# Softmax maxima two chunks ahead, and tile factors at the last block, in a convolution with a mixture of experts

## The chip, the core and the metric

The kernel runs on one core of a Trainium2 chip. A core has five engines that work side by side, each with its own queue of instructions: TensorE (PE, with its weight loads shown as PEld), VectorE (DVE), ScalarE (ACT), GpSimd (POOL) and SyncE (SP), which here only issues transfers. The metric is the time of one execution on the device in microseconds. The time before is the median of 3 runs; the profile is of one further execution.

## What is computed

Two layers follow each other. The first is a causal convolution with 7 taps whose weights are given for each position and head and go through a softmax; the second sends each of the 28672 rows to one of 8 experts, a two-layer network with a ReLU between.

```python
# x: (8, 3584, 192), weight_gen: (8, 3584, 8 heads, 7 taps)
w = weight_gen - np.max(weight_gen, axis=-1, keepdims=True)
w = np.exp(w)
w = w / (np.sum(w, axis=-1, keepdims=True) + 1e-09)
out = np.einsum('bshk,bskhg->bshg', w, x_unf)      # 7 shifted copies of x
...
logits = x @ w_gate                                # (28672, 192) @ (192, 8)
expert_idx = np.argmax(logits, axis=1)
gate_w = probs[np.arange(N), expert_idx]           # softmax of the logits
h = np.maximum(x_sorted[lo:hi] @ w1[e], 0.0)       # (rows, 192) @ (192, 1024)
y_sorted[lo:hi] = h @ w2[e]                        # (rows, 1024) @ (1024, 192)
return gate_w[:, None] * y
```

## The kernel before

**Chunks.** The rows are cut into 28 chunks of 1024 (8 rows on each of 128 partitions). For each chunk `load` brings `x_sb` and `w_sb` (three buffers of each) and the convolution runs on DVE. `soft1` takes the maximum over 7 taps on DVE (L323, `mx`), subtracts it on POOL (L324) and takes the exponential on ACT (L325), all in place in `w_sb`; `soft2` sums on DVE (L330, `sm`), scales (L332) and takes the reciprocal (L335); `soft3` multiplies the weights by it into `wp` in PSUM (L342). `taps` then multiplies and adds (L351, L375): for chunks from 3 on these are 7 multiplications and 6 additions, one instruction each, so that with `soft3` a chunk has 14 steps. The generator `sums` (L660) counts them in `n`: squares of the next chunk (ACT, L407) are written at n = 1 and 2, `soft1` of the next chunk at n = 2, and from n = 4 (`SC_AT`) one instruction of `scale` (L416 to L423, which needs the squares) and `soft2` of the next chunk follows each step. Multiplications read `wp` from PSUM; additions read two operands from SBUF.

**From a chunk to the experts' queues.** `split` makes two half-precision parts of the result and transposes them on PE (L471, copied by ACT at L473). `finish` computes the logits on PE, picks the expert and the gate value on DVE (L492 to L544, the last of them `pos`), and `send` scatters the 1024 rows to the experts' queues in HBM with 8 indirect transfers on POOL (L559, `queue<-pl,pos`).

**Tiles.** `choose` picks full tiles of 256, later 384 rows of one expert as soon as a queue has them; what is left after the last chunk goes in tiles of 384, 256, 128 and fewer rows. There are 97 tiles. `fetch` (L711) issues for a tile, on SP, the rows `xt` (L736), the expert's weights `wt` (L738, three buffers, so a tile's weights wait for the second layer of the tile three before it) and the small table `meta` with gate value and row number (L741). `experts` (L747) computes a tile in blocks of inner units: 8 blocks for 384 rows, 4 for 256, 2 for 128, 1 for 64 and fewer. A block is 5 matmuls per 128 inner units (L797), then a ReLU into `hh` on ACT and its remainder `hl`, on DVE (L820) or, for every third tile (n % 3 = 1), by PE and ACT (L806, L810, L812). Between the blocks of a tile stand the second layer's matmuls (L704) of the tile before it. Each 128 rows of that layer end in `o` (L708, ACT), scaled by the tile's factors `fac`, and a scatter to the output on POOL (L559, `out_dram<-o,meta`).

**The factors.** `fac` (L834, ACT, four buffers) is the table's gate value times a constant that lies with the expert's weights. It is written once per tile, after the first block's ReLU, and first read by the tile's `o`, whose instructions are written among the blocks of the next tile.

**Order.** DVE's order is written out by hand (`tc.manual_schedule`): `vector_step` interleaves the remainders `hl`, the route of a chunk, its split and the steps of `sums` by a clock that is kept in the program. The queues of the other engines are laid out when the kernel is built, by a planner that gives an engine its next instruction from those whose data and buffers it takes to be ready. On the chip each engine then takes its queue in that order and waits where the data are not there.

Of the kernel before, what the change touches and what calls it, by code (L numbers as in the profile page):

```python
# [11 lines left out]
F16 = mybir.dt.float16  # L12
# [7 lines left out]
P = 128  # L20
# [11 lines left out]
J = 8  # L32
# [1 line left out]
HELP = 3  # L34
EARLY = 5
STEP = 0.2
REST = 10.0
REST0 = 12.0
HURRY = 0.3
SOON = 4  # L40
BY_PE = 28
REST1 = 6.0
START = 20.0
AHEAD = 7
# [11 lines left out]
T_MAIN = 384  # L56
CIN = 3
T_STEP = 16
SC_AT = 4
SQ = 4  # L60
PROB = 3
TV = 2
# [51 lines left out]
def conv_moe_kernel(ctx: ExitStack, tc: tile.TileContext, x, wgen, w_gate, w1, w2, out):  # L114
# [202 lines left out]
    ssqs = const.tile([P, 2, J // 2], F32, name="ssqs")  # L317
    nc.vector.memset(ssqs, 0.0)

    def soft1(c):  # L320
        k = ch[c]
        mx = cw.tile([P, J * H], F32, name="mx")
        nc.vector.tensor_reduce(mx, k.w, axis=AX.X, op=ALU.max)  # L323
        nc.gpsimd.tensor_tensor(k.w, k.w, mx.unsqueeze(2).to_broadcast([P, J * H, KW]), op=ALU.subtract)  # L324
        nc.scalar.activation(k.w, k.w, AF.Exp)  # L325

    def soft2(c):
        k = ch[c]
# [120 lines left out]
    def low(c):  # L449
        k = ch[c]  # L450
        p16 = k.pl.bitcast(F16)
        h = k.pc or J // 2
        sub_ = dict(op=ALU.subtract)
        for a, b in ((h, J),) if k.pc else ((0, h), (h, J)):
            nc.vector.tensor_tensor(p16[:, a:b, 2 * P:3 * P], k.acc[:, a:b, 0:P], p16[:, a:b, 0:P], **sub_)
            yield 0.0, (b - a) * 0.14 + 0.08
            nc.vector.tensor_tensor(p16[:, a:b, D:D + 64], k.acc[:, a:b, P:D], p16[:, a:b, P:D], **sub_)
            if b < J:
                yield 0.0, 0.4
        k.lsc = rt.tile([P, 1], F32, name="lsc")  # L460
        nc.vector.tensor_tensor(k.lsc, k.isx, gi, op=ALU.mult)
        xg = cw.tile([P, 4 * J, P], I16, name="xg", bufs=SPLITS)
        k.xg = xg.bitcast(F16)
        k.nb = 3 if c < BY_PE else 4
        if c < BY_PE:

            blocks = [(j, n) for j in range(J) for n in range(3)]
            for i in range(0, len(blocks), 8):
                pt = ps_h.tile([P, 8, P], F16, name="ph")
                for m, (j, n) in enumerate(blocks[i:i + 8]):  # L470
                    nc.tensor.transpose(pt[:, m, :], p16[:, j, n * P:(n + 1) * P], idh)  # L471
                    clock[1] += P / 2400.0 + MM
                nc.scalar.activation(k.xg[:, i:i + 8, :], pt, AF.Copy)  # L473
        else:
            nc.sync.dma_start_transpose(xg, k.pl.bitcast(I16).rearrange("p j d -> p (j d)"))
        k.sent = clock[0] + 0.4
        yield 0.0, 0.4

    def logits(c):
        k = ch[c]  # L480
        k.pm = ps_m.tile([P, 512], F32, name="pm")
        k.lp = k.pm[:, 0:J * 2 * E].rearrange("p (j t e) -> p j t e", j=J, t=2)
        for j in range(J):
            for n in range(3):
                nc.tensor.matmul(k.lp[:, j], k.xg[:, k.nb * j + n, :], gw[:, n], start=(n == 0), stop=(n == 2))
                clock[1] += GATE

    def route1(c):
# [157 lines left out]

    def finish(c):

        yield max(0.0, ch[c].sent + (REST1 if c < BY_PE else REST0 if c < SOON else REST) - clock[0])
        logits(c)  # L650
        yield from route1(c)
        ranks(c)
        yield from gate(c)
        yield from places(c)
        send(c)
        if c == NCH - 1:
            pad_queues()
        yield from choose(c)

    def sums():  # L660

        soft1(0)
        x0 = ch[0].x
        nc.vector.tensor_scalar(x0[:, 0:HALO, :], x0[:, 0:HALO, :], inner, None, op0=ALU.mult)
        square(0, 0, J)
        yield 0.6, None
        for d in chain(scale(0), soft2(0)):
            yield d, None
        for c in range(NCH):
            if c + 2 < NCH:  # L670
                load(c + 2)
            n = 0
            side = iter(())
            for cost in taps(c):
                n += 1
                if n <= 2 and c + 1 < NCH:
                    for i in range(4 * n - 4, 4 * n, SQ):
                        square(c + 1, i, SQ)
                yield cost, None
                if c + 1 < NCH:  # L680
                    if n == 2:
                        soft1(c + 1)
                        yield 0.6, None
                    if n == SC_AT:
                        side = chain(scale(c + 1), soft2(c + 1))
                d = next(side, None)
                if d is not None:
                    yield d, None
            for d in side:
                yield d, None  # L690
            yield 0.0, c
# [55 lines left out]
    def experts():  # L747
# [25 lines left out]
        while True:  # L773
            go = yield n, 0.0
            if not go:
                break
            while len(done_) < min(n + 2, len(todo)):
                loaded[len(done_)] = fetch(len(done_))
                done_.append(len(done_))
            T, xt, wt, meta = loaded.pop(n)  # L780
            fac = ffx.tile([P, 4], F32, name="fac", bufs=4)
            hh = ffh.tile([P, NF, T], F16, name="hh", padded_shape=[P, NF, T_MAIN])
            hl = ffh.tile([P, NF, T], F16, name="hl", padded_shape=[P, NF, T_MAIN])
            fg = max(g for g in (1, 2, 4, 8) if g * T <= 512 or g == 1)
            groups = NF // fg
            for t in range(groups):
                if t:
                    yield None, 0.0
                f0 = t * fg
                flush()  # L790
                while len(pend) > 3:
                    low_part()
                ph = ps_h.tile([P, fg, T], F32, name="ph")
                for g in range(fg):
                    f = f0 + g
                    for k, (wc, xc) in enumerate(((0, 0), (0, 2), (O_L0, 0), (O_H1, 1), (O_L1, 1))):
                        nc.tensor.matmul(ph[:, g], wt[:, wc + f * P:wc + (f + 1) * P], xt[:, xc, 0:T],  # L797
                                         start=(k == 0 and g == 0), stop=(k == 4),
                                         skip_group_check=g > 0)
                hv, lv = hh[:, f0:f0 + fg], hl[:, f0:f0 + fg]  # L800
                while subs:
                    subs.pop(0)()
                if (n % 3 == 1 or todo[n][3] < EARLY) and todo[n][3] < NCH - 1:


                    nc.scalar.activation(hv, ph, AF.Relu, scale=SHRINK)  # L806

                    def rest(ph=ph, hv=hv, lv=lv, fg=fg):
                        for g in range(fg):
                            nc.tensor.matmul(ph[:, g], negi, hv[:, g], start=False, stop=True,  # L810
                                             skip_group_check=True)
                        nc.scalar.activation(lv, ph, AF.Relu)  # L812

                    subs.append(rest)
                    clock[1] += T * fg * (6 + 4.5) / 2400.0 + 15 * fg * MM
                else:
                    nc.scalar.activation(hv, ph, AF.Relu)  # L817

                    def lo(ph=ph, hv=hv, lv=lv):
                        nc.vector.scalar_tensor_tensor(lv, ph, 0.0, hv, op0=ALU.max, op1=ALU.subtract)  # L820
                        return (T * fg + 60) / 960.0

                    cost = T * fg * (5 + 4.5) / 2400.0 + 14 * fg * MM
                    clock[1] += cost
                    pend.append((clock[1] + LATE, n, lo))
                if t > 0 or groups == 1:
                    while pend and pend[0][1] < n:
                        low_part()
                    m = -(-left // (groups - t))
                    second(m)  # L830
                    left -= m
                if t == 0:
                    p = min(P, T)
                    nc.scalar.activation(fac[0:p, 0:T // p], meta[0:p, 0:T // p, 0], AF.Copy,  # L834
                                         scale=wt[0:p, O_INV:O_INV + 2].bitcast(F32))
                if t >= 1 and len(done_) < len(todo):
                    m = len(done_)
                    if m <= n + 2 or (todo[m][3] == NCH - 1 and m <= n + AHEAD + 2):
                        loaded[m] = fetch(m)
                        done_.append(m)  # L840
            while subs:
                subs.pop(0)()
            second(10 ** 6)
            prev = l2(T, hh, hl, wt, meta, fac)
            left = -(-T // P) * NF * 3
            n += 1
# [149 lines left out]
```

## Time and profile before

| | |
|---|---|
| time of the runs | 1338.81, 1340.34, 1341.35 us (median 1340.34) |
| time of the profiled execution | 1336.57 us |
| its span, first to last instruction | 1334.9 us |
| PE busy | 1166.3 us (87%) |
| DVE busy | 1044.7 us (78%) |
| ACT busy | 715.4 us (54%) |
| POOL busy | 588.2 us (44%) |
| granted TensorE clock, mean | 0.954 |

Busy time is the union of an engine's instructions; an instruction that waits is not busy. The views group instructions as `line engine operation out<-in`, with buffer numbers left out. In a view of waits a row reads `engine line <- what ended the wait: us in total, times, longest`; in a timeline a row reads `start, duration, engine, line, operation, out<-in, shapes, count`, and in square brackets how long the engine had stood idle before it and what ended that. In the table of busy time by stretch a row reads `from:to length`, then for each engine its busy time and its number of instructions, then the granted clock, the share of the transfer engines and GB/s. `SPq` marks an instruction of SyncE's queue that issues a transfer.

### The profile page before, as it was taken

Reading aid. Unit: us, or ns where it says so; the run is one execution under the profiler, and the core shown is the slowest. Engines: PE = TensorE matmul, PEld = TensorE weight load, DVE = VectorE, ACT = ScalarE, POOL = GpSimd, SP = SyncE. Lnnn points to the kernel's source line nnn. Section 1 sums busy time; section 2 is a strip of 40 time slices with the busy share of each in tenths; the row PEclk is TensorE's granted clock in tenths of the full one; section 3 lists DMA queues with packets and bytes.
Section 4 is the critical chain, followed back from the end, with each engine's and each line's share of the span. In section 5 each row is a group of like instructions: output and inputs, shape, how many; then the busy total and the mean of one; then the engine's idle time right before and its main releaser. Section 6 shows DMA issues by size and latency. Waiting matters only on the chain.

```text
span 1334.9 us, 30220 instructions
## 1 busy us (share of the span) xinstructions
PE 1166.3 (87%) x11621; PEld 943.3 (71%) x11621; DVE 1044.7 (78%) x1888; ACT 715.4 (54%) x1590; POOL 588.2 (44%) x520
## 2 busy tenths in 40 slices
PE   5673689795889999899989889999999999899997
PEld 3452579684667777677766677777777777679997
DVE  7979698898898898888987888998989996233331
ACT  3644457664556555556645555665655545443442
POOL 2033454544445545355453655444554647322222
PEclk9887799896999999999999999999999999999999
DMA  9996786847466766676666667766666666999995
GB/s 268 297 328 204 241 258 234 257 139 249 130 192 195 216 226 190 188 203 221 221 188 181 200 197 207 238 190 199 209 228 181 190 209 207 297 370 323 312 332 225
DMA packets 185134, 305.02 MB, mean 228 GB/s; under 512 B 132752, under 2 KB 156434, under 8 KB 172574
## 3 DMA queue, kind: packets, MB, share of 16 engines
q1 hardware_dynamic: 162862, 257.76, 61.8%
q0 software_dynamic: 22128, 45.33, 10.6%
q8 instruction: 91, 1.49, 0.4%
q14 instruction: 53, 0.43, 0.1%
HBM read 220.24 MB, written 60.76 MB: 211 GB/s over the span
## 4 chain that ended last, share of the span: by engine, by line
PE 33%; DMA 26%; DVE 14%; issue 10%; POOL 9%; ACT 6%; SPq 2%; POOLq 0%; DVEq 0%; ACTq 0%
DMA meta<-queue 15%; PE ph L797 15%; PE y L704 15%; DMA queue<-pl,pos 5%; POOL queue L559 4%; DVE acc L375 4%; DVE tv L351 4%; POOL out_dram L559 3%; DMA wt<-wq 3%; DVE hl L820 2%; DMA f<-in_moe_w_dram 1%; ACT xg L473 1%; POOL w_sb L324 1%; DMA out_dram<-o,meta 1%; PE ph L810 1%
## 5 line engine op out<-in xcount | busy, mean ns | idle before, releaser
L797 PE MATMUL ph<-xt,wt 128*128 128x384 f16 (+6 forms) x3880 | 590.8, 296 | 39.6 <-DMA xt<-queue 20.6
L704 PE MATMUL y<-wt,hh 128*128 128x192 f16 (+2 forms) x3696 | 516.6, 249 | 26.7 <-ACT o L708 25.3
L559 POOL DMA_INDIRECT out_dram<-o,meta x231 | 270.5, 1171 | 523.6 <-ACT o L708 471.3
L704 PE MATMUL y<-wt,hl 128*128 128x192 f16 (+2 forms) x1848 | 455.8, 249 | 0.9 <-DVE hl L820 0.5
L797 PEld LDWEIGHTS <-wt 128*128 128x128 f16 x3880 | 333.7, 99 | 165.9 <-issue 46.7
L704 PEld LDWEIGHTS <-hh 128*128 128x128 f16 (+2 forms) x3696 | 341.1, 99 | 76.9 <-issue 42.7
L820 DVE SCALAR_TENSOR_TENSOR hl<-ph,hh 128x384 f16<-128x384 f32 (+2 forms) x372 | 206.2, 562 | 200.7 <-ACT hh L817 195.6
L559 POOL DMA_INDIRECT queue<-pl,pos x224 | 276.3, 1234 | 163.0 <-issue 61.8
L351 DVE TENSOR_TENSOR tv<-x_sb,wp 128x1536 f32<-128x1536 f32 (+1 forms) x171 | 287.5, 1685 | 4.9 <-PE ph L360 4.7
L375 DVE TENSOR_TENSOR acc<-acc,tv 128x1536 f32<-128x1536 f32 x150 | 266.2, 1774 | 0.1
L817 ACT ACTIVATE hh<-ph 128x384 f16<-128x384 f32 (+2 forms) x372 | 179.4, 500 | 117.1 <-PE ph L797 104.7
L704 PEld LDWEIGHTS <-hl 128*128 128x128 f16 (+2 forms) x1848 | 183.4, 99 | 19.9 <-ACT hl L812 1.6
L806 ACT ACTIVATE hh<-ph 128x384 f16<-128x384 f32 (+1 forms) x204 | 104.4, 520 | 53.4 <-PE ph L797 49.4
L708 ACT ACTIVATE o<-y,fac 128x192 f32<-128x192 f32 (+2 forms) x231 | 91.9, 420 | 71.9 <-PE y L704 71.5
L834 ACT ACTIVATE fac<-meta,wt 128x3 f32<-128x3 f32 (+6 forms) x97 | 28.7, 296 | 189.6 <-DMA meta<-queue 189.0
L812 ACT ACTIVATE hl<-ph 128x384 f16<-128x384 f32 (+1 forms) x204 | 102.9, 521 | 23.5 <-PE ph L810 23.0
L473 ACT ACTIVATE xg<-ph 128x1024 f16<-128x1024 f16 x84 | 82.9, 1023 | 12.0 <-PE ph L471 11.9
L810 PE MATMUL ph<-hh,negi 128*128 128x384 f16 (+1 forms) x256 | 69.8, 310 | 19.4 <-ACT hh L806 19.4
L471 PE MATMUL ph<-idh,pl 128*128 128x128 f16 x672 | 57.6, 236 | 16.2 <-ACT pl L442 7.2
L471 PEld LDWEIGHTS <-pl 128*128 128x128 f16 x672 | 48.1, 107 | 20.2 <-ACT pl L442 7.6
L360 PE MATMUL ph<-tv,identf 128*128 128x384 f32 x126 | 50.0, 538 | 8.0 <-DVE tv L351 7.9
L407 ACT ACTIVATE junk<-x_sb 128x768 bf16<-128x768 f32 (+2 forms) x56 | 48.2, 861 | 10.9 <-DMA x_sb<-in_x_dram 5.4
(120 smaller groups left out, 785.2 us busy)
## 6 DMA issues: line engine op xcount, KB each, us to landing
wt<-wq SPq DMA_DIRECT2D x97, 1796.0 KB
x_sb<-in_x_dram SPq DMA_DIRECT2D x28, 768.0 KB
w_sb<-in_weight_gen_dram SPq DMA_DIRECT2D x28, 224.0 KB
wq<-ws SPq DMA_DIRECT2D x8, 772.0 KB
f<-in_moe_w_dram SPq DMA_DIRECT2D x8, 768.0 KB
f<-in_moe_w_dram SPq DMA_DIRECT2D x8, 512.0 KB
wq<-ws SPq DMA_DIRECT2D x8, 512.0 KB
wq<-ws SPq DMA_DIRECT2D x32, 128.0 KB
```

The source lines that it names most:

```text
L351: eng.tensor_tensor(out, xs, ws, op=ALU.mult)
L375: eng.tensor_tensor(ac, ac, t, op=ALU.add)
L471: nc.tensor.transpose(pt[:, m, :], p16[:, j, n * P:(n + 1) * P], idh)
L473: nc.scalar.activation(k.xg[:, i:i + 8, :], pt, AF.Copy)
L559: st = nc.gpsimd.indirect_dma_start(out=dst, out_offset=bass.IndirectOffsetOnAxis(ap=idx, axis=0), in_=src, in_offset=None, **kw)
L704: nc.tensor.matmul(y, hx[:, f, sl], w2v[:, f, t, :], start=(f == 0 and k == 0), stop=(f == NF - 1 and k == 2))
L708: nc.scalar.activation(o[0:m, :], y, AF.Copy, scale=fac[0:m, s:s + 1])
L797: nc.tensor.matmul(ph[:, g], wt[:, wc + f * P:wc + (f + 1) * P], xt[:, xc, 0:T], start=(k == 0 and g == 0), stop=(k == 4), skip_group_chec ...
L806: nc.scalar.activation(hv, ph, AF.Relu, scale=SHRINK)
L812: nc.scalar.activation(lv, ph, AF.Relu)
L817: nc.scalar.activation(hv, ph, AF.Relu)
L820: nc.vector.scalar_tensor_tensor(lv, ph, 0.0, hv, op0=ALU.max, op1=ALU.subtract)
```

## The change

`soft1` is cut in two. `soft0` holds the maximum and the subtraction, `soft1` the exponential alone. For the first chunks (up to chunk 4) `soft0` stays at step 2 of the chunk before; from chunk 5 on it is written at step 11 (`MX_AT`) of the chunk two before. The exponential is written at step 4 instead of 2 of the chunk before, and `scale` and `soft2` begin at step 7 instead of 4. In `experts` the factors are written after the tile's last block instead of its first. The transposing transfer for chunks from `BY_PE` on goes, with its constants, and `xg` holds 24 blocks instead of 32.

```diff
-REST = 10.0
-REST0 = 12.0
-BY_PE = 28
-SC_AT = 4
+MX_AT = 11
+EXP_AT = 4
+SC_AT = 7
+MX_FROM = 3
...
-    def soft1(c):
+    def soft0(c):
         k = ch[c]
         mx = cw.tile([P, J * H], F32, name="mx")
         nc.vector.tensor_reduce(mx, k.w, axis=AX.X, op=ALU.max)
         nc.gpsimd.tensor_tensor(k.w, k.w, mx.unsqueeze(2).to_broadcast([P, J * H, KW]), op=ALU.subtract)
-        nc.scalar.activation(k.w, k.w, AF.Exp)
+
+    def soft1(c):
+        nc.scalar.activation(ch[c].w, ch[c].w, AF.Exp)
...
-        xg = cw.tile([P, 4 * J, P], I16, name="xg", bufs=SPLITS)
-        k.xg = xg.bitcast(F16)
-        k.nb = 3 if c < BY_PE else 4
-        if c < BY_PE:
...
-        else:
-            nc.sync.dma_start_transpose(xg, k.pl.bitcast(I16).rearrange("p j d -> p (j d)"))
+        k.xg = cw.tile([P, 3 * J, P], F16, name="xg", bufs=SPLITS)
...
-        yield max(0.0, ch[c].sent + (REST1 if c < BY_PE else REST0 if c < SOON else REST) - clock[0])
+        yield max(0.0, ch[c].sent + REST1 - clock[0])
...
     def sums():
 
+        soft0(0)
         soft1(0)
...
                 if c + 1 < NCH:
-                    if n == 2:
+                    if n == 2 and c + 1 < MX_FROM + 2:
+                        soft0(c + 1)
+                        yield 0.6, None
+                    if n == EXP_AT:
                         soft1(c + 1)
+                    if n == MX_AT and MX_FROM <= c < NCH - 2:
+
+                        soft0(c + 2)
                         yield 0.6, None
                     if n == SC_AT:
                         side = chain(scale(c + 1), soft2(c + 1))
...
-                if t == 0:
+                if t == groups - 1:
+
                     p = min(P, T)
                     nc.scalar.activation(fac[0:p, 0:T // p], meta[0:p, 0:T // p, 0], AF.Copy,
                                          scale=wt[0:p, O_INV:O_INV + 2].bitcast(F32))
```

More of the change, by code (lines that the diff above doesn't have):

```diff
@@ L461, in low @@
         nc.vector.tensor_tensor(k.lsc, k.isx, gi, op=ALU.mult)
-        xg = cw.tile([P, 4 * J, P], I16, name="xg", bufs=SPLITS)
-        k.xg = xg.bitcast(F16)
-        k.nb = 3 if c < BY_PE else 4
-        if c < BY_PE:
[L467 to L473, printed above, removed]
-        else:
-            nc.sync.dma_start_transpose(xg, k.pl.bitcast(I16).rearrange("p j d -> p (j d)"))
+        k.xg = cw.tile([P, 3 * J, P], F16, name="xg", bufs=SPLITS)
+        blocks = [(j, n) for j in range(J) for n in range(3)]
+        for i in range(0, len(blocks), 8):
+            pt = ps_h.tile([P, 8, P], F16, name="ph")
+            for m, (j, n) in enumerate(blocks[i:i + 8]):
+                nc.tensor.transpose(pt[:, m, :], p16[:, j, n * P:(n + 1) * P], idh)
+                clock[1] += P / 2400.0 + MM
+            nc.scalar.activation(k.xg[:, i:i + 8, :], pt, AF.Copy)
         k.sent = clock[0] + 0.4
@@ L484, in logits @@
             for n in range(3):
-                nc.tensor.matmul(k.lp[:, j], k.xg[:, k.nb * j + n, :], gw[:, n], start=(n == 0), stop=(n == 2))
+                nc.tensor.matmul(k.lp[:, j], k.xg[:, 3 * j + n, :], gw[:, n], start=(n == 0), stop=(n == 2))
                 clock[1] += GATE
```

## The prediction

> **What bounds the kernel now.** I read the page's first part, then busy time by stretch, because the run has two stages: up to about 1110 us the convolution on DVE and the experts on PE share the core; after that only expert tiles are left.
>
> ```profile
> span 1334.9 us, 30220 instructions
> 150.00:1110.00 960.00, 870.80 (x8504) 698.37 (x8502) 837.37 (x1459) 557.73 (x1270) 474.04 (x389) 0.96 0.67 204
> 1110.00:1335.00 225.00, 211.47 (x2566) 188.01 (x2564) 75.86 (x167) 90.20 (x210) 71.44 (x74) 0.99 0.90 303
> ```
>
> The columns are PE, PEld, DVE, ACT, POOL, clock, DMA. In the long stage PE is busy 91% and DVE 87%, with 89.2 and 122.6 us idle; ACT is busy only 58%. No engine is full: PE and DVE take turns waiting, and the views of ACT's and DVE's waits (150 to 1110 us) say for whom.
>
> ```profile
> ACT fac L834 <- DMA meta<-queue: 137.0, 58, 6.0
> ACT w_sb L325 <- POOL w_sb L324: 65.0, 19, 6.6
> DVE hl L820 <- ACT hh L817: 64.7, 41, 5.1
> DVE sm L330 <- ACT w_sb L325: 14.5, 4, 6.2
> ```
>
> ACT takes its instructions in order. It stands 137.0 us before a tile's factors (their table `meta` has not landed) and 65.0 us before the softmax exponential (POOL has not subtracted the maximum). Behind it wait the blocks' `hh`, and DVE stands 64.7 us for those and 14.5 us for the exponential itself. The last stage starts when the last chunk is sent; an edit to the softmax can only bring that moment forward.
>
> What a wait costs the other engines is read from stretches from where ACT stops to 2.5 us after it goes on: 19 of them for the exponential (first, last, sum), 55 for the factors (sum).
>
> ```profile
> 239.34:245.52 6.18, 2.81 (x24) 2.38 (x23) 2.53 (x5) 2.50 (x6) 5.21 (x5) 0.88 0.45 131
> ...
> 1036.31:1041.34 5.03, 4.45 (x39) 3.11 (x37) 5.03 (x9) 2.23 (x8) 4.53 (x4) 1.00 0.78 167
> sum 112.48, PE 73.62 PEld 54.87 DVE 64.50 ACT 44.34 POOL 76.11; mean PE 3.88 PEld 2.89 DVE 3.39 ACT 2.33 POOL 4.01
> sum 272.81, PE 232.44 PEld 181.39 DVE 241.37 ACT 119.97 POOL 116.35; mean PE 4.23 PEld 3.30 DVE 4.39 ACT 2.18 POOL 2.12
> ```
>
> Exponential: DVE idles 112.5 - 64.5 = 48.0 us and PE 38.9. At the stage's own rates (12.8% and 9.3%) it would be 14.4 and 10.4, so these waits cost 33.6 us of DVE and 28.4 of PE. Factors: DVE idles 31.4 us, 11.5%, no more than everywhere; PE 40.4, which is 15.1 over its rate. So the wait that is half as long costs more.
>
> **The dead branch.** There are 28 chunks and `BY_PE` is 28, so every chunk already goes through PE and `REST1`. That branch, its constants and a quarter of the `xg` buffer go at no cost in either direction.
>
> **The factors.** The instruction is the same; it is only written down 7 blocks later (1 to 3 in smaller tiles). What counts is where it then stands in ACT's queue, and the trace shows that the written place does not decide this. DVE alone keeps its written order; the other queues are laid out by the planner.
>
> ```profile
> 1010.47 0.38 SPq L741 DMA_DIRECT2D meta<-queue  x1
> 1015.26 0.49 ACT L806 ACTIVATE hh<-ph 128x384 f16<-128x384 f32 x1 [0.32 <-PE ph L797]
> 1019.26 0.30 ACT L834 ACTIVATE fac<-meta,wt 128x3 f32<-128x3 f32 x1 [3.51 <-DMA meta<-queue]
> ...
> 1284.16 0.42 ACT L708 ACTIVATE o<-y,fac 128x192 f32<-128x192 f32 x1 [1.38 <-PE y L704]
> 1284.61 0.29 ACT L834 ACTIVATE fac<-meta,wt 128x1 f32<-128x1 f32 x1
> ```
>
> The load at 1010.47 is the 60th (tile 59), and so is the factor at 1019.26. The block before it is L806, the form of tiles with n % 3 = 1, so tile 58: the factors stand a whole tile ahead of their written place, 5.3 us of ACT's time behind the issue of their load (1019.26 - 3.51 - 1010.47), which lands 8.8 us after it. At the end they stand right behind an `o`, the instruction that frees one of their four buffers. Both places are the earliest that data and buffers allow. So is this one:
>
> ```profile
> 500.11 0.15 DVE L416 TENSOR_REDUCE ssq<-ssqs 128x1 f32<-128x8 f32 x1
> 504.68 0.83 ACT L407 ACTIVATE junk<-x_sb 128x768 bf16<-128x768 f32 x1
> 526.79 0.61 DVE L342 TENSOR_TENSOR wp<-w_sb,sm 128x448 f32<-128x448 f32 x1
> ```
>
> The sum at 500.11 uses up the squares of chunk 14; those at 504.68 are chunk 15's, written after 526.79: 22 us early. A planner that takes what is ready leaves the factors where they are. I take 0 us; the other end is 15 (PE's excess) to 40 us (all of PE's idle there) of gain. The move adds no wait: if the written place did hold, the factors would come after the tile's eighth block, and the first `o` of a tile is written in the next tile, so nothing would wait for them.
>
> **The softmax.** Maximum, subtraction and exponential are neither added nor removed; DVE's order really changes. One chunk as it is now:
>
> ```profile
> 485.31 0.62 DVE L342 TENSOR_TENSOR wp<-w_sb,sm 128x448 f32<-128x448 f32 x1
> 493.93 0.60 DVE L323 TENSOR_REDUCE mx<-w_sb 128x64 f32<-128x448 f32 x1
> 500.56 2.23 POOL L559 DMA_INDIRECT out_dram<-o,meta  x1 [0.30 <-issue]
> 502.77 1.02 POOL L324 TENSOR_TENSOR w_sb<-w_sb,mx 128x448 f32<-128x448 f32 x1
> 503.82 0.58 ACT L325 ACTIVATE w_sb<-w_sb 128x448 f32<-128x448 f32 x1 [4.22 <-POOL w_sb L324]
> 512.82 0.61 DVE L330 TENSOR_REDUCE sm<-w_sb 128x64 f32<-128x448 f32 x1
> 519.52 1.75 DVE L375 TENSOR_TENSOR acc<-acc,tv 128x1536 f32<-128x1536 f32 x1
> 520.77 1.36 POOL L559 DMA_INDIRECT out_dram<-o,meta  x1 [2.65 <-ACT o L708]
> 521.39 1.74 DVE L351 TENSOR_TENSOR tv<-x_sb,wp 128x1536 f32<-128x1536 f32 x1
> 525.35 2.23 POOL L559 DMA_INDIRECT queue<-pl,pos  x1 [3.22 <-DVE pos L544]
> ```
>
> The maximum is done at 494.5, but POOL is in the chunk's burst of scatters and subtracts at 502.8, 8.3 us later; ACT had stood since 499.6. Step 11 is the addition at 519.5, so the new maximum stands at about 521.2. POOL is then nearly free: one scatter ends at 522.1, and it idles 3.2 us before the next burst. The subtraction runs there, for a chunk whose sums come a whole chunk later, and `sm` (step 10 instead of 7) finds its data: the 14.5 us go.
>
> The maxima move past no DMA of their own, but need their weights sooner.
>
> ```profile
> L303 SPq DMA_DIRECT2D w_sb<-in_weight_gen_dram x21: 338/339/676, 159.6 to 942.3; - x21
> L323 DVE TENSOR_REDUCE mx<-w_sb x23: 596/600/615, 155.4 to 1029.7; 128x64 f32<-128x448 f32 x23
> ```
>
> The last load is issued at 942.3 and its maximum stands at 1029.7, step 2 of a chunk; it moves to step 11 of the chunk before, 14 us earlier by the chunk above (521.2 to 493.9 plus the 41.5 us between two `wp`). Some 70 us are left: no price.
>
> The exponential will be laid out behind the subtraction, wherever it is written, so its wait shrinks rather than vanishes. The nearest row for ACT waiting on a result of DVE in this stage:
>
> ```profile
> ACT eg L498 <- DVE lg L497: 11.1, 11, 1.9
> ```
>
> That is 11.1 / 23 = 0.5 us a chunk; with POOL between I take 0.8 us where it is 65.0 / 23 = 2.8 now, bounds 0 and 2.8. So 71% goes. On DVE: 14.5 + 0.71 x (33.6 - 14.5) = 28 us; on PE 0.71 x 28.4 = 20. The stage needs both engines: 24 us.
>
> Against it stands what POOL does to DVE.
>
> ```profile
> 539.11 1.74 DVE L351 TENSOR_TENSOR tv<-x_sb,wp 128x1536 f32<-128x1536 f32 x1
> 539.82 1.02 POOL L324 TENSOR_TENSOR w_sb<-w_sb,mx 128x448 f32<-128x448 f32 x1
> ...
> 1037.30 3.14 DVE L375 TENSOR_TENSOR acc<-acc,tv 128x1536 f32<-128x1536 f32 x1
> 1037.80 1.01 POOL L324 TENSOR_TENSOR w_sb<-w_sb,mx 128x448 f32<-128x448 f32 x1
> L375 DVE TENSOR_TENSOR acc<-acc,tv x150: 1728/1747/3139, 116.7 to 1099.0; 128x1536 f32<-128x1536 f32 x150
> ```
>
> An addition under a subtraction took 3.14 us instead of 1.75: 1.39 lost. The multiplication under one took its usual 1.74. Now DVE often idles while POOL subtracts; after the change it runs. The new maximum is followed by a multiplication (1.74 us, free), then two additions. If POOL comes late each time, the price is 23 x 1.39 = 32 us; if at once, 0. POOL was at most one scatter away above, so I take 4.
>
> The Trainium skill, "SBUF — State Buffer", section "Who interferes with whom", has this as a rule against the change: a DVE instruction with two SBUF inputs and a GpSimd instruction that reads SBUF exclude each other, whoever is second waits. The trace agrees (3.14 against 1.75 us). By the rule alone a subtraction beside the multiplication (one input in PSUM) would cost nothing and one beside an addition up to its own 1.0 us.
>
> **Sum.** 24 - 4 = 20 us. The profiled execution took 1336.57 us for its 1334.9 us span; the median of the runs is 1340.34. So 1320 us.
>
> **The rivals.**
> 1. *The written place of the factors holds.* Against: their places above. Then 15 to 40 us more, say 28: 1292.
> 2. *The wait only moves.* The exponential keeps 2.8 us because the subtraction falls among the next burst, released 4 us after the new maximum; or what ACT gains there it stands before the next factors, 3.51 us instead of less. For: the burst's closeness. Price: 14.5 us at most is kept, the port takes some: 1340.
> 3. *Slower: the subtraction lands on the additions.* POOL comes 1.7 us or more after the maximum in every chunk, and each costs 1.39 us: 32 us lost, while a late POOL leaves only the 14.5 us of the gain: 17.5 slower, 1358. It decides once the loss exceeds 14.5 / 23 = 0.63 us a chunk. For: the 3.14 us; against: POOL's gap.
>
> **The numbers.** Forecast 0.60 (its own range 1305 to 1333), rival 1 0.12, rival 2 0.13, rival 3 0.15. Measurements of this kernel tell 0.2%, 2.7 us, from no change. Faster 0.60 + 0.12 = 0.72, same 0.13, slower 0.15. The range leaves out the far halves of rivals 1 and 3: 1286 to 1346.
>
> **What would show it.** Right: factors still stand before `meta` for about 137 us in this stage; the exponential's wait is some 20 us; `sm` waits for nothing; the last chunk's convolution ends some 20 us sooner and the last stage keeps its 225 us. Wrong: factors behind their own tile's blocks with no wait (rival 1); subtractions 8 us after the maximum (2); L375's median unchanged but some twenty additions near 3 us (3).

## Result and profile after

The changed kernel took 1301.43 us (median of 4 runs, 1294.43 to 1308.22) against 1340.76 us before it on the same chip: a ratio of 0.9709, 95% interval 0.9656 to 0.9762. The profiled execution took 1300.56 us, 36.0 less than that of before (1336.57). The forecast was 1320: the direction was right, and the gain was twice as large. The time lies outside the forecast's own range (1305 to 1333) and inside the whole range (1286 to 1346).

Busy time by stretch of the kernel before and of the changed kernel (columns PE, PEld, DVE, ACT, POOL, clock, DMA, GB/s). So that the same work lies in the long stage of both, each is cut here where the last chunk's last `pos` on DVE ends, at 1115.87 us before and 1079.47 us now:

```profile
150.00:1115.87 965.87, 876.67 (x8567) 702.94 (x8565) 840.36 (x1475) 562.02 (x1280) 478.43 (x393) 0.96 0.67 204
1115.87:1334.87 219.00, 205.60 (x2503) 183.44 (x2501) 72.86 (x152) 85.92 (x198) 67.05 (x69) 0.99 0.91 303
```

```profile
150.00:1079.47 929.47, 859.54 (x8508) 690.36 (x8508) 841.12 (x1474) 557.50 (x1271) 496.84 (x393) 0.97 0.70 211
1079.47:1298.85 219.38, 208.59 (x2532) 186.16 (x2530) 72.95 (x153) 86.53 (x201) 66.35 (x69) 0.99 0.92 307
```

The last stage kept its length (219.0 us before, 219.4 now), so everything came from the long stage, which is 36.4 us shorter. DVE is busy as long there as before (840 and 841 us), so its idle time had to fall by about as much: from 125.5 to 88.3 us, by 37.2. That is bookkeeping, and it doesn't show that DVE alone is the bound. PE's idle time fell from 89.2 to 69.9 us, by 19.3, and its busy time by 17.1. Over the whole execution PE's 11621 matmuls took 1153.9 us instead of 1166.3, at a mean granted clock of 0.964 instead of 0.954.

The waits of the long stage (150 to 1075 us), of ACT and DVE and then of POOL (us, times, longest):

```profile
ACT fac L838 <- DMA meta<-queue: 168.1, 62, 10.0
ACT w_sb L327 <- POOL w_sb L324: 18.1, 11, 5.0
...
DVE hl L823 <- ACT hh L820: 48.2, 28, 6.4
...
POOL w_sb L324 <- DVE mx L323: 19.4, 9, 3.6
```

The exponential's wait for POOL fell from 65.0 to 18.1 us, and `sm` has no row any more (14.5). In its place POOL now stands 19.4 us for the maximum. The factors stand longer than before, 168.1 us against 137.0. One chunk in order of time (start, us, then idle time before it and what ended it):

```profile
490.68 0.61 DVE L332 TENSOR_REDUCE sm<-w_sb 128x64 f32<-128x448 f32 x1
491.27 1.75 DVE L377 TENSOR_TENSOR acc<-acc,tv 128x1536 f32<-128x1536 f32 x1
493.08 0.61 DVE L323 TENSOR_REDUCE mx<-w_sb 128x64 f32<-128x448 f32 x1
493.78 1.04 POOL L324 TENSOR_TENSOR w_sb<-w_sb,mx 128x448 f32<-128x448 f32 x1 [2.29 <-DVE mx L323]
494.86 0.58 ACT L327 ACTIVATE w_sb<-w_sb 128x448 f32<-128x448 f32 x1
...
500.14 1.09 POOL L555 DMA_INDIRECT queue<-pl,pos  x1 [1.35 <-DVE pos L540]
```

POOL is free when the maximum comes and subtracts 0.1 us after it; before it was 8.3 us in the chunk shown. The exponential follows at once, although it is written a chunk later, and the sum of the next chunk (490.68) finds its exponential long done. Not every chunk is like this one. Of the 23 subtractions that moved, by the starts of L323 and L324 in the trace, 16 begin within 1.4 us of the end of their maximum and 7 between 2.7 and 13.0 us after it; before the change the 23 began 2.7 to 14.3 us after it, half of them 6.6 us or more.

### The profile page after: what moved, and what is told of

It is laid out like the page before. It is cut to its first block, busy times and chain, and to the rows that moved or that the text cites. A ratio compares the mean times of both kernels' runs of the same rounds, so it can differ in the third digit from the quotient of the medians.

```text
span 1298.8 us, 30225 instructions
## 1 busy us (share of the span) xinstructions
PE 1153.9 (89%) x11621; PEld 933.7 (72%) x11621; DVE 1045.9 (81%) x1888; ACT 714.5 (55%) x1590; POOL 606.2 (47%) x520
## 4 chain that ended last, share of the span: by engine, by line
PE 35%; DMA 33%; DVE 9%; ACT 8%; issue 8%; POOL 4%; SPq 2%; POOLq 0%; ACTq 0%; DVEq 0%
DMA meta<-queue 25%; PE ph L800 16%; PE y L707 16%; POOL queue L555 3%; DVE tv L353 3%; DMA queue<-pl,pos 2%; DVE acc L377 2%; ACT hh L820 1%; DMA wt<-wq 1%; PE ph L813 1%; DVE hl L823 1%; ACT o L711 1%; PE ph L469 1%; ACT xg L471 1%; POOL out_dram L555 1%
## 5 line engine op out<-in xcount | busy, mean ns | idle before, releaser
L800 PE MATMUL ph<-xt,wt 128*128 128x384 f16 (+6 forms) x3880 | 584.9, 295 | 35.8 <-DMA xt<-queue 30.2
L707 PE MATMUL y<-wt,hh 128*128 128x192 f16 (+2 forms) x3696 | 502.8, 247 | 26.9 <-ACT o L711 25.4
L555 POOL DMA_INDIRECT out_dram<-o,meta x231 | 285.6, 1236 | 470.0 <-ACT o L711 422.3
L707 PE MATMUL y<-wt,hl 128*128 128x192 f16 (+2 forms) x1848 | 449.9, 247 | 1.8 <-ACT hl L815 1.0
L707 PEld LDWEIGHTS <-hh 128*128 128x128 f16 (+2 forms) x3696 | 337.4, 99 | 65.0 <-issue 32.6
L377 DVE TENSOR_TENSOR acc<-acc,tv 128x1536 f32<-128x1536 f32 x150 | 263.2, 1755 | 0.1
L324 POOL TENSOR_TENSOR w_sb<-w_sb,mx 128x448 f32<-128x448 f32 x28 | 29.9, 1067 | 69.7 <-DVE mx L323 67.8
L409 ACT ACTIVATE junk<-x_sb 128x768 bf16<-128x768 f32 (+2 forms) x56 | 48.3, 862 | 19.0 <-issue 10.1
```

The source lines that it names most:

```text
L377: eng.tensor_tensor(ac, ac, t, op=ALU.add)
L555: st = nc.gpsimd.indirect_dma_start(out=dst, out_offset=bass.IndirectOffsetOnAxis(ap=idx, axis=0), in_=src, in_offset=None, **kw)
L707: nc.tensor.matmul(y, hx[:, f, sl], w2v[:, f, t, :], start=(f == 0 and k == 0), stop=(f == NF - 1 and k == 2))
```

## Experiments

The runs went to several chips, and the kernel before doesn't take the same time on all of them. On some it took 1338 to 1341 us, as in the first comparison (called A here), on two others 1406 and 1407 (called B). Ratios are to the kernel before on the same chip, and numbers are compared within a kind. Expectations that give times were written for the times of A. "Tap n" in the expectations is step n of a chunk.

| kernel | chip | median us | ratio, 95% interval |
|---|---|---|---|
| changed kernel, first comparison | A | 1301.43 | 0.9709 (0.9656 to 0.9762) |
| softmax part only | B | 1385.95 | 0.9833 (0.9787 to 0.9879) |
| factors written last, only | B | 1407.23 | 1.0012 (0.9977 to 1.0047) |
| changed, factors held behind last block | B | 1353.62 | 0.9619 (0.9580 to 0.9659) |
| changed, sums back at step 4 | B | 1397.70 | 0.9943 (0.9916 to 0.9971) |
| changed kernel again | B | 1381.14 | 0.9795 (0.9724 to 0.9865) |
| before, sums at step 7 | B | 1402.58 | 0.9974 (0.9941 to 1.0007) |
| changed, maxima at step 2 | B | 1407.88 | 1.0028 (0.9994 to 1.0063) |
| before, factors held behind last block | B | 1397.31 | 0.9942 (0.9911 to 0.9972) |
| changed, maximum at 2, subtraction at 11 | A | 1313.45 | 0.9795 (0.9758 to 0.9833) |
| changed, maximum at 11, subtraction at 2 | A | 1320.73 | 0.9849 (0.9813 to 0.9884) |
| changed, factors held behind first block | A | 1245.70 | 0.9276 (0.9241 to 0.9311) |
| before, factors held behind first block | A | 1327.12 | 0.9918 (0.9902 to 0.9935) |

**The two parts apart.** The softmax part alone is the changed kernel with the factors where they were; the factors alone are the kernel before with one line changed:

```diff
-                if t == 0:
+                if t == groups - 1:
```

> The changed kernel with the factors written back after the first block. My theory (the written place of the factors decides nothing, the softmax is the whole gain): 1301 us like the changed kernel, within its own spread of 1294 to 1308, and ACT still stands 160 to 170 us before the factors in the long stage. Rival (the surplus over my forecast comes from the factors): 1320 us.

> The kernel before with only the factors' instruction written after the last block. My theory: the planner puts it where it was, 1340 us, ACT's wait before the factors in 150 to 1110 us stays at 137 us. Rival (the written place holds): the wait goes to under 20 us and the time to between 1300 and 1325 us.

> The changed kernel once more, beside the three others of this batch. If the gain of the first comparison (ratio 0.971) is that of the kernel, the ratio lies between 0.965 and 0.98; if it was partly the chip's, it lies at 0.983, where the softmax part alone came out beside the factors held. The exponential's wait on POOL's subtraction is about 20 us between 150 and 1080 us, and the factors wait over 100 us for their meta load.

The written place of the factors does nothing: the kernel before with that line has the same order of instructions on every engine, and its ratio is 1.0012. The softmax part alone differs from the changed kernel in two places of ACT's order and nowhere else, and the two (0.9833 and 0.9795) agree within their intervals. The factors' wait for `meta` (150 to 1150 us) is 113.5 us in the softmax part alone and 114.1 with only the factors' line changed, less than the 160 to 170 and 137 that were expected from A; the changed kernel has 110.2 on B. Its own ratio, 0.9795, fits both cases of its expectation. The gain is smaller on B than on A: the softmax part's interval (0.9787 to 0.9879) lies clear of that on A (0.9656 to 0.9762), though the changed kernel's own on B (0.9724 to 0.9865) still overlaps it. A row of the kernel with only the factors' line changed (150 to 1150 us) shows less to be won on B:

```profile
ACT w_sb L325 <- POOL w_sb L324: 24.4, 7, 5.1
DVE sm L330 <- ACT w_sb L325: 12.2, 3, 6.2
```

The exponential stands 24.4 us for POOL where on A it stood 65.0.

**Maxima and sums apart.** The change has two moves on DVE, the maxima to step 11 and the sums to step 7. Each was made alone, and then both with the maximum a chunk further ahead but at step 2:

```diff
 # sums back (changed kernel)
-EXP_AT = 4
-SC_AT = 7
+EXP_AT = 2
+SC_AT = 4
 # sums later (kernel before)
-SC_AT = 4
+SC_AT = 7
 # maxima at step 2 (changed kernel)
-MX_AT = 11
+MX_AT = 2
```

> The changed kernel with the factors after the first block, the exponential written at step 2 and the sums from step 4 as before: only maximum and subtraction stand a chunk earlier. My theory (the gain is the exponential's wait for POOL and the 14.5 us of the sums, both of which go when the subtraction is a chunk early): 1301 us, ACT's wait before the exponential about 20 us in the long stage, no wait of the sums. Rival (the later sums carry a third or more of the gain): 1312 us or more.

> The kernel before with its sums, scales and squares moved from tap 4 to tap 7 of a chunk and nothing else: the maxima stay at tap 2, the subtraction and the exponential right behind them. If the early maxima carry the gain, the wait of the exponential on POOL stays at 24 us or more and the ratio is 0.995 to 1.003. If the later sums carry it (two thirds of the gain went when they were put back at tap 4), the ratio is 0.985 to 0.99 although that wait stays. If the two only work together, the ratio is 1.0 and the wait stays, but the sums no longer wait for the exponential.

> The changed kernel with its maxima at tap 2 in place of tap 11 of the chunk two ahead: nine taps earlier, still a chunk ahead of the exponential, but inside the stretch in which the additions and POOL's routing of the chunk run. If only the distance from maximum to exponential counts, the time is that of the changed kernel within 0.3%. If the place of the subtraction beside the additions counts (port), the additions' mean goes from 1755 ns up to 1776 ns or more and the time is up by 4 to 10 us. If POOL's routing work holds the subtraction back but the distance covers it, the subtraction starts over 3 us behind its maximum in most chunks and the time doesn't move.

The maxima alone give 0.6%, the later sums alone 0.3% (their interval takes in no change), the two together about 2%, and the maxima at step 2 nothing at all. The first is a miss: the whole gain was expected of the maxima alone, and although the exponential's wait was as short as expected and `sm` had no wait, two thirds of the gain stayed away. Of the later sums the third case came. Of the maxima at step 2 none of the three did. The rows of sums later, of maxima at step 2, of the changed kernel on the same chip and of the maxima alone (150 to 1150 us):

```profile
DVE hl L820 <- ACT hh L817: 107.8, 45, 9.0
ACT w_sb L325 <- POOL w_sb L324: 22.2, 6, 7.0
```

```profile
DVE hl L823 <- ACT hh L820: 110.4, 47, 7.1
ACT w_sb L327 <- POOL w_sb L324: 18.1, 7, 6.4
```

```profile
DVE hl L823 <- ACT hh L820: 81.6, 29, 7.6
ACT w_sb L327 <- POOL w_sb L324: 17.3, 9, 5.0
```

```profile
DVE hl L823 <- ACT hh L820: 65.4, 35, 8.6
ACT w_sb L327 <- POOL w_sb L324: 19.5, 14, 5.6
```

The exponential's wait is much the same in all four, so on B it is not what tells a kernel with a gain from one without. DVE's wait for `hh` doesn't tell either: it is some 110 us with the maximum and the subtraction among the chunk's first steps and 82 with both at step 11, but least of all, 65.4, in the maxima alone, which gained only 0.6%. The ratios show that it matters on B where the softmax work stands, and not only how far ahead (1.003 at step 2, 0.980 at step 11); which wait carries that is not shown. The expectation had the place only by way of the additions, and their mean, wanted at 1776 ns or more, was 1743.

**Whose place: the maximum's on DVE, or the subtraction's on POOL?** `soft0` was cut once more, and the subtraction made to wait for a multiplication or addition of a later step. In the first kernel DVE keeps exactly the order of "maxima at step 2", in the second that of the changed kernel; the planner laid out the queues of ACT, POOL and PE anew in both:

```diff
-        nc.gpsimd.tensor_tensor(k.w, k.w, mx.unsqueeze(2).to_broadcast([P, J * H, KW]), op=ALU.subtract)
+        k.mx = mx
+
+    def soft0b(c, tap):
+        k = ch[c]
+        sub = nc.gpsimd.tensor_tensor(k.w, k.w, k.mx.unsqueeze(2).to_broadcast([P, J * H, KW]), op=ALU.subtract)
+        if tap:
+            tc.add_manual_dep(sub.ins, tap[-1].ins.name, wait_for, reason="subtraction behind the tap")
...
 # maximum at 2, subtraction at 11
+                    if n == 2 and MX_FROM <= c < NCH - 2:
+                        soft0(c + 2)
+                    if n == MX_AT and MX_FROM <= c < NCH - 2:
+                        soft0b(c + 2, tapped)
 # maximum at 11, subtraction at 2 of the next chunk
+                    if n == 2 and c + 1 >= MX_FROM + 2:
+                        soft0b(c + 1, tapped)
+                    if n == MX_AT and MX_FROM <= c < NCH - 2:
+                        soft0(c + 2)
```

> The changed kernel with the maximum two chunks ahead taken at tap 2, in the chunk's burst, and the subtraction made to wait for tap 11: VectorE's order is that of the kernel with maxima at tap 2 (ratio 1.003 to before), POOL subtracts where the changed kernel does (0.980). If the place of the maximum in VectorE's order decides, the ratio is 0.998 to 1.005. If the place of the subtraction on POOL and of the exponential on ScalarE decides, it is 0.976 to 0.985. Between 0.985 and 0.998 both have a part. By the prediction's reasoning (the wait of the exponential on POOL carries the gain) the ratio is at most 0.985, since that wait is not above that of the changed kernel, 17 us.

> The other way round: the maximum at tap 11 of the chunk two ahead, as in the changed kernel and with VectorE's order unchanged, and the subtraction made to wait for tap 2 of the next chunk, in POOL's and ScalarE's burst, a chunk's taps ahead of the sums. If VectorE's order decides, the ratio stays at 0.976 to 0.985 although POOL and ScalarE do the softmax in the burst. If the place on POOL and ScalarE decides, it is 0.995 to 1.003. By the prediction's reasoning the wait of the exponential on POOL comes back to 22 us or more, and the ratio with it to 0.99 to 1.0.

They ran on A, where the changed kernel stands at 0.971. The long stage, cut at the last `pos` as above, and the exponential's wait (150 to 1110 us) of maximum at 2, subtraction at 11:

```profile
150.00:1086.89 936.89, 861.53 (x8540) 690.40 (x8538) 842.68 (x1474) 560.92 (x1280) 469.61 (x393) 0.98 0.70 210
...
ACT w_sb L336 <- POOL w_sb L331: 15.6, 10, 3.2
```

and of maximum at 11, subtraction at 2:

```profile
150.00:1097.26 947.26, 866.62 (x8529) 695.15 (x8528) 841.08 (x1474) 558.78 (x1276) 492.56 (x393) 0.97 0.69 207
...
ACT w_sb L336 <- POOL w_sb L331: 57.9, 21, 7.2
```

Neither place decides alone. With the subtraction in the burst the exponential's wait comes back (57.9 us), as the prediction's reasoning said, but the ratio is 0.985 and not 0.99 to 1.0: half of the gain stays. That kernel has no `sm` row either, and DVE idles 947.26 - 841.08 = 106.2 us, 19.3 less than before. The 14.5 us that DVE stood for `sm` would make most of that; they were not taken away by themselves. From there to the changed kernel (88.3) it is another 17.8 us of DVE, for 57.9 - 18.1 = 39.8 us of the exponential's wait. With the maximum at 2 and the subtraction at 11 DVE idles 94.2 us, 5.9 more than in the changed kernel, with as small a wait; the two ratios' intervals (0.9758 to 0.9833, 0.9656 to 0.9762) just touch. So on A about half of the gain goes with the subtraction's place and the exponential's wait, the other half stays without it and fits `sm`, and a small part may need the maximum out of the first steps. What the new order of the other queues adds was not separated.

**The factors really held.** An order on ACT, without a semaphore, keeps a tile's factors behind its block's ReLU. The two forms differ in whether the factors are written after the last block (`t == groups - 1`) or the first (`t == 0`); both were also put on the kernel before:

```diff
+    behind = mybir.DependencyInfo(mybir.DependencyClass.NoSync, mybir.DependencyReason.DATA)
...
-                    nc.scalar.activation(hv, ph, AF.Relu)
+                    last = nc.scalar.activation(hv, ph, AF.Relu)
...
-                    nc.scalar.activation(fac[0:p, 0:T // p], meta[0:p, 0:T // p, 0], AF.Copy,
-                                         scale=wt[0:p, O_INV:O_INV + 2].bitcast(F32))
+                    made = nc.scalar.activation(fac[0:p, 0:T // p], meta[0:p, 0:T // p, 0], AF.Copy,
+                                                scale=wt[0:p, O_INV:O_INV + 2].bitcast(F32))
+                    tc.add_manual_dep(made.ins, last.ins.name, behind, reason="factors behind the block's relu")
```

> The changed kernel with an order edge that really holds the factors behind the last block's ReLU of their tile on ACT. Both theories: ACT's wait before the factors in the long stage falls from 168 us to under 20 us. If those waits cost what PE's idle time in them says (15 to 40 us): 1261 to 1286 us. If they cost DVE nothing and DVE's end of the convolution sets the time: 1301 us. Slower than 1301 only if the first o of the next tile has to wait for the factors.

> The kernel before with the factors written behind the last block, and an order on ScalarE that keeps them there, and no softmax part. If the waits of the factors cost as the rival of the prediction says, this alone gives what it gave on top of the softmax part, a ratio of 0.975 to 0.98, and the wait of the factors on the meta load is 0. If ScalarE's waits for meta only take the place of others while VectorE still waits for the exponential, the ratio is 0.995 to 1.0 and the wait of the exponential on POOL grows from 24 us to 60 us.

> The changed kernel with the factors held on ScalarE behind their tile's first block in place of its last. If the wait for the meta load is what costs, and its absence what made the kernel with factors behind the last block 2.3% faster than the softmax part alone, the factors wait under 10 us here too and the ratio is that of the other, 0.958 to 0.966. If the place at the last block matters (factors out of the way of the tile's first blocks), the ratio is 0.966 to 0.98.

> The kernel before with the factors held on ScalarE behind their tile's first block, and no softmax part: what the factors' place is worth in the kernel that the prediction was made from, which took it to be 15 to 40 us (ratio 0.989 to 0.970 of 1340 us). If the hold and the softmax part add up, the ratio is that of the kernel with both divided by that of the changed kernel, 0.955 where before takes about 1340 us. If ScalarE, freed of the meta waits, then stands for POOL's subtraction instead, the ratio is 0.985 to 1.0 and the exponential's wait on POOL is at least that of before, 65 us. Where before takes about 1406 us, the hold at the last block alone gave 0.994: a ratio there within 0.005 of that says that the block doesn't matter.

In none of the four has the factors' wait for `meta` a row left. On top of the softmax part that makes the fastest kernel of this study: 1245.7 us, 0.9276 of before and 4.3 points under the changed kernel, more than either case of the expectation (0.958 to 0.966, 0.966 to 0.98). Behind the last block, on B, the hold took 27.5 us off the changed kernel's median (1381.14 to 1353.62). Alone, the edit gives 0.8% behind the first block on A and 0.6% behind the last on B. What a factor did to ACT is seen in the order of time of the changed kernel:

```profile
914.83 0.49 ACT L820 ACTIVATE hh<-ph 128x384 f16<-128x384 f32 x1 [0.38 <-PE ph L800]
918.92 0.30 ACT L838 ACTIVATE fac<-meta,wt 128x3 f32<-128x3 f32 x1 [3.60 <-DMA meta<-queue]
919.12 1.23 ACT L820 ACTIVATE hh<-ph 128x384 f16<-128x384 f32 x3
```

Three blocks' `hh` have piled up behind the factors. Held behind the first block, the factors at about the same time wait for nothing; the stage and its waits (150 to 1026 us) follow:

```profile
916.62 0.49 ACT L821 ACTIVATE hh<-ph 128x384 f16<-128x384 f32 x1 [1.78 <-PE ph L801]
917.01 0.29 ACT L839 ACTIVATE fac<-meta,wt 128x3 f32<-128x3 f32 x1
917.19 0.34 ACT L494 ACTIVATE eg<-lg,lsc 128x64 f32<-128x64 f32 x1
...
150.00:1027.42 877.42, 848.51 (x8529) 688.76 (x8527) 837.70 (x1474) 570.53 (x1274) 498.44 (x393) 0.98 0.73 223
...
ACT w_sb L327 <- POOL w_sb L324: 17.6, 10, 5.8
DVE hl L824 <- ACT hh L821: 10.1, 10, 2.4
```

DVE's wait for `hh` in the stage is 10.1 us where it was 48.2, and its idle time 877.42 - 837.70 = 39.7. Without the softmax part, the stage and its waits (150 to 1110 us) are these:

```profile
150.00:1110.97 960.97, 877.66 (x8565) 704.87 (x8564) 838.10 (x1475) 570.74 (x1281) 476.71 (x394) 0.95 0.68 205
1110.97:1328.97 218.00, 203.47 (x2503) 182.57 (x2501) 73.17 (x152) 85.26 (x198) 67.52 (x69) 0.99 0.94 304
...
ACT w_sb L325 <- POOL w_sb L324: 95.3, 21, 8.8
DVE hl L821 <- ACT hh L818: 59.4, 29, 6.6
DVE sm L330 <- ACT w_sb L325: 14.5, 4, 6.2
```

ACT no longer stands for `meta`, comes to the exponential earlier and stands there, 95.3 us instead of 65.0. The long stage is 4.9 us shorter and DVE idles 960.97 - 838.10 = 122.9 us in it, only 2.6 less than before. The two parts alone are worth 2.9 and 0.8 points, together 7.2. On A the two waits, which stand in one queue, thus cover each other at least in part: 30 of the 137 us that ACT no longer stands for `meta` come back at the exponential. Two things keep this from being the whole account. The granted clock was lower in the executions of this kernel (0.945 to 0.950, against 0.953 to 0.959 of the kernel before on the same chip), and what that costs was not separated. And on B, behind the last block, the hold gives 0.6% alone and 1.8 points on top of the change, while the exponential's wait hardly grew (24.4 to 26.9 us where the expectation had 60).

Over the profiled executions on A, with every stage cut at the last `pos` (965.87 us long before, with 125.5 us of idle time on DVE and 89.2 on PE; the execution took 1336.57):

| kernel (A) | long stage | change | DVE idle there | change | PE idle there | change of the execution's time |
|---|---|---|---|---|---|---|
| changed | 929.5 | -36.4 | 88.3 | -37.2 | 69.9 | -36.0 |
| maximum at 2, subtraction at 11 | 936.9 | -29.0 | 94.2 | -31.3 | 75.4 | -25.1 |
| maximum at 11, subtraction at 2 | 947.3 | -18.6 | 106.2 | -19.3 | 80.6 | -15.6 |
| changed, held behind first block | 877.4 | -88.5 | 39.7 | -85.8 | 28.9 | -83.7 |
| before, held behind first block | 961.0 | -4.9 | 122.9 | -2.6 | 83.3 | -5.8 |

In all five the gain is made in the long stage; the last stage is up to 4.8 us longer than before in three of them. DVE's work in the stage is nearly the same in all (837.7 to 842.7 us), so its idle time has to fall with the stage. PE's idle time falls with it too, by less.

**What stays open.** Whether the first block is a better place than the last: the two forms with the softmax part ran on different kinds of chip (0.9276 on A, 0.9619 on B). Why the maxima at step 2 keep nothing on B, while the kernel on A with the same order on DVE and the subtraction at step 11 keeps two thirds: either the subtraction's place or the chip. Whether the higher granted clock of the changed kernel (0.960 to 0.968 over its executions, 0.947 to 0.959 for the kernel before on such chips) made part of the gain or came with it. The dead branch was not taken out by itself.

## Why the prediction was right and wrong

- **The bound.** Right. The gain is all in the stage that DVE and PE share, and the last stage kept its length. The sum took 24 us because "the stage needs both engines", between 28 for DVE and 20 for PE. PE's 20 was right as a number (its idle time fell by 19.3), but PE's busy time also fell, so its idle time is no measure of the stage here. DVE's work stayed the same, and its idle time is. The average cost 4 us.
- **The softmax mechanism.** Right: the wait of the exponential fell by 72% (71% forecast), that for `sm` went, and the exponential runs far ahead of its written place, 19 to 37 us before its sums. That the size came out so close is in part luck: the forecast had 0.8 us in every chunk, and the 18.1 us came from 11 waits of up to 5.0.
- **Its price, the step that failed.** Beside `sm` the 65.0 us of the exponential's wait were priced at 33.6 - 14.5 = 19.1 us of DVE, 0.29 for each microsecond. With the subtraction put back into the burst DVE idles 17.8 us more for 39.8 us more of that wait, 0.45 for each, and DVE's gain over the whole change was 37.2 and not 28. As far as the figures show, what was wrong is the rate that was taken off. The 19 stretches were charged only with idle time above the stage's own rate of 12.8%, a rate that these waits and those for `meta` had themselves raised: in the fastest kernel it is 39.7 / 877.4 = 4.5%. With 4.5% the same 19 stretches cost 48.0 - 5.1 = 42.9 us, and the prediction's line gives 14.5 + 0.71 x (42.9 - 14.5) = 34.7. That the stretches end 2.5 us after ACT goes on matters little: ended 6 us after it, they hold 57.3 us of DVE's idle time in 179.0, which is 34.4 above 12.8%. The miss adds up: 9 us by this price, 4 by the average and 4 set aside for the port are 17, and the stage got 36.4 - 20 = 16.4 us shorter than forecast.
- **The port.** 4 us were set aside for subtractions that land on additions. That loss did not come: 2 of the 150 additions took over 2 us (both 2.84), where 5 had before, and their mean went from 1774 to 1755 ns, over 150 of them a gain of 3 us. Their durations in the changed kernel (min, median, max):

```profile
L377 DVE TENSOR_TENSOR acc<-acc,tv x150: 1682/1748/2844, 113.7 to 1059.6; 128x1536 f32<-128x1536 f32 x150
```

  POOL came at once in the chunk shown, in the gap between its bursts, and not while an addition ran. The rule of the Trainium skill that the prediction weighed ("SBUF — State Buffer", section "Who interferes with whom") spoke against the change with the additions alone, and the 1748 ns of the median and the 1.04 us of the subtraction shown agree that where the two don't meet nothing is lost. What the prediction took from that section, that whoever is second waits, the traces bear out only in part: the two do exclude each other, but in the row it showed the addition began first (1037.30), took 3.14 us, and the subtraction that began 0.50 us later ran its usual 1.01. The changed kernel has both outcomes: an addition at 936.08 took 2.83 us with a subtraction of 1.00 us from 936.29, and beside an addition of 1.70 us at 536.41 a subtraction from 536.98 took 1.94.
- **The factors.** That the written place decides nothing was right; the 0 us stands. Their worth, 15 to 40 us in the first rival, was wrong in both directions. In the kernel before, the hold gives 11 us (1338.09 to 1327.12), while the exponential's wait grows from 65.0 to 95.3. Once that wait is mostly gone it gives 4.3 points, 56 us between the two medians (1301.43 and 1245.70). The prediction had read from the 55 stretches that DVE idles there no more than everywhere and so loses nothing. "Everywhere" held the same waits: without them the stage's rate for DVE is 4.5%, not 12.8%. Taken against that, the 55 stretches cost 31.4 - 12.3 = 19.1 us of DVE, still well short of the 48.6 us by which the hold cut DVE's idle time on top of the softmax part (88.3 to 39.7). Why it is worth that much is not shown.
- **The rivals.** None came. The first had times of 1280 to 1305 us, and the 1301.43 lies among them, but not by its mechanism: the factors still stand for `meta`, 168.1 us. The whole range reached down to 1286 only for this rival, so that it holds the measured time is luck. The slower rival needed POOL 1.7 us late in every chunk; it was in 7 of 23. "The wait only moves" was right about a small part: the meta wait grew from 137.0 to 168.1 us, but that grew out of time ACT had won, while the kernel got faster.
- **The signs named.** The exponential's wait of some 20 us: 18.1. `sm`: no wait. The last stage: kept. The convolution's end 20 us sooner: 36.5, as the last `wp` moved from 1064.2 to 1027.7. The factors' 137 us: not kept, 168.1.

## What to carry to other kernels

When an engine that takes its instructions in order stands for two things in the same stretch, price neither wait by itself: here they were worth 2.9 and 0.8 points alone and 7.2 together. Don't take a stage's own idle rate as the rate without loss when the wait in question makes up much of that rate: here 12.8% gave 28 us, and 4.5%, known only from a later run, gives 35 where 37 were measured. When one engine's work stays the same and another's doesn't, count a stage's gain by the idle time of the first. And where a planner lays out a queue, writing an instruction later can move nothing; here an order on its own engine did, and it is worth trying on a small instruction that stands for a small load.

## What the runs showed that was not expected

The same program takes 1338 to 1341 us on some chips and 1406 to 1407 on others. On the slower ones PE's records have gaps with nothing to wait for; the kernel with only the factors' line changed, whose order is that of before, shows them there (150 to 1180 us):

```profile
PE ph L471 <- issue: 13.2, 20, 1.2
PE ph L797 <- issue: 12.2, 14, 2.5
PE pm L485 <- issue: 8.2, 13, 1.2
PE y L704 <- issue: 6.9, 13, 1.8
```

They come to about 41 us; the medians of the kernel before lie 65 us apart (1406.24 and 1340.76). The profiles on the faster chips have no such row for PE. The clock was lower as well (0.923 to 0.942 over the executions of the kernel before there, 0.947 to 0.959 on A). What makes the gaps was not found. By the medians the same softmax change was worth 2.9% on one chip and 1.7 to 2.1% on the two others.
